# Half of K computed by seven products beside w2's, kept in DRAM and loaded back in attention

## The chip, the cores and the metric

One core of a Trainium2 chip runs the whole program. The metric is the device time of one execution in microseconds (us); a kernel's time is the median of several runs. The core's engines work at the same time and meet through semaphores: TensorE (PE) multiplies and writes into the eight accumulator banks, VectorE (DVE) and ScalarE (ACT) read the banks and do elementwise work, GpSimd (POOL) does some elementwise work, and SyncE (SP) issues nearly all DMAs. Each engine takes its instructions in the order in which the program gives them; an instruction that waits holds up everything behind it on that engine.

## What is computed

The reference, cut to what matters here (x has 2048 rows of 1024, four segments of 512 rows; 32 heads of 32; F is 3584):

```python
xn = _layernorm(A_x, axis=-1)
# branch A, attention with a memory that goes from segment to segment
q, k, v = xn @ wq, xn @ wk, xn @ wv                # split into heads and segments
for s in range(N):
    logits = einsum('bhqd,bhkd->bhqk', qs, ks) * scale + mask
    p = softmax(logits); a_dot = p @ vs
    pq = phi(qs)                                   # t + 1 where t > 0, else exp(t)
    a_mem = (pq @ M) / (pq @ z + 1e-6)
    o = g * a_mem + (1.0 - g) * a_dot              # g = sigmoid(beta)
    pk = phi(ks); M = M + pk.T @ vs; z = z + pk.sum()
A = o @ wo
# branch B, an MLP over the rows
h = _layernorm(xn); u = gelu(einsum('bsd,sf->bdf', h, w1) + b1)
B = transpose(einsum('bdf,fs->bds', u, w2) + b2)
out = x + A + B
```

## The kernel before

The kernel is one Python program that gives instructions to the engines in the order in which it runs; the class FW adds the semaphore waits (L134) from what each instruction reads and writes. There is no other scheduler: the order of the calls is the order on every engine.

**Hidden layer and w2.** `norm_and_first_hidden` loads x, normalises it chunk by chunk (a chunk is 128 rows, `N_TCH` = 16 of them) and multiplies the first two column blocks. A few matmuls on zeros run ahead of it (`N_WARM`, L389). `products` (about L703) then works through 20 *pairs*: 12 of w1 (indices 0 to 11) and 8 of w2 (12 to 19, called w2 pairs 0 to 7 here). A pair is a product of 2 by 2 blocks in seven block products instead of eight, in the order 1, 6, 5, 7, 2, 4, 3 (`ORDER`). Left operands are blocks of the weights or one of four sums of them (`sums`, on VectorE), right operands are blocks of the activations or one of four differences (`differences`, VectorE). A product of w2 is 14 matmuls of 512 columns. Three banks take a pair's results: X products 1 and 2, Y products 6, 7 and 4, Z products 5 and 3. Between them banks are read while they go on accumulating: ScalarE copies X after product 1 (`copy_bank`), VectorE adds Y to that copy after product 6 and after product 7 (`add_bank`, L690), so product 7 can start only when the add after product 6 has read Y. `after2` finishes w2's results (L934), stores them as partial outputs, loads the next w2 columns, and issues the next pair's four sums, one after each of products 7, 2, 4 and 3. The sums of consecutive w2 pairs lie in two sets in turn (`alloc_s2`).

**x for attention.** x is loaded again chunk by chunk (`xn_load`), normalised on VectorE (`xn_scale`, L986) and transposed by a DMA (`xn_transpose`) into xnT. Two buffers xs take the chunks in turn, so a load waits until the transpose of two chunks before has landed. Chunks 0 to 3 go through in w2 pairs 0 to 3, one a pair; the other twelve in attention, in the first four units of segments 0 to 2.

**Attention.** `attention` (about L1354) runs over 32 *units*; a unit is four heads of one segment, units 0 to 7 are segment 0, 8 to 15 segment 1 and so on. Each unit has logits (row-packed matmuls into banks 0 to 3, an exp on ScalarE, L1216, a mask on GpSimd, L1220), and the weighing of V by the unit before's probabilities in three parts (`weigh`, banks 4 and 5, read out by VectorE, L1267). Between these pieces `dense` puts matmuls of *jobs*, eight 512-column matmuls each, in banks 6 and 7 in turn: q and k of the unit after next, one of V's chunks, and output products wo of an earlier segment. `unit_jobs` says which; `cut` divides them among the gaps. k is copied out by VectorE (L1112), q by ScalarE (L1103). VectorE's other work (`combine`, L1298 to L1320, `phi_q` and `phi_k`, L1080 and L1082, scaling x) stands in a list `side`; one piece of it is issued whenever a job reaches one of its *stops* (`STOPS`, after matmuls 1, 4 and 7, or 1 and 4 where VectorE reads the job's bank). `wo_plan` says in which units the output products stand. `tail` does the last segment's output products, in the banks of a fixed list.

Of the kernel before, what the change touches and what calls it, by code (L numbers as in the profile page):

```python
# [105 lines left out]
class FW:  # L106
    N_DMA_SEMS = 64
    N_OUT_SEMS = 44
    N_OWN_SEMS = 16
# [275 lines left out]
class _Kernel:  # L385
# [3 lines left out]
    N_WARM = 12  # L389
# [314 lines left out]
    def products(self):  # L704
        fw = self.fw
        g = _Walk(self.mem, self.G_AT, self.B_AT)
        for b in range(8):
            if b == 0:
                self.alloc_hidden(g)
            self.gelu(b // 2, b % 2, self.bank(b), self.R_bank[b])  # L710
        self.h_diff((1, 2))
        self.pairs = {}
        n1 = self.N_W1
        order = [(0, 1), (1, 1), (0, 2), (1, 2), (0, 6), (0, 5), (0, 7), (1, 6), (0, 4), (1, 5), (1, 7), (0, 3), (1, 4), (1, 3)]
        order += [(i, p) for i in range(2, n1 + self.N_W2) for p in self.ORDER]
        self.later = deque()
        for i, p in order:
            if i not in self.pairs:
                self.begin_pair(i)
            pair = self.pairs[i]  # L720
            self.product(pair, p)
            pair.done.add(p)
            (self.after1 if i < n1 else self.after2)(pair, p)
# [29 lines left out]
    def begin_pair(self, i):  # L753
        n1 = self.N_W1
        banks = [(3 * i + j) % 8 for j in range(3)]
        if i < n1:
            slot, R_slot, s, R_s, n = self.w1s[i % 2], self.R_w1s[i % 2], self.s1[i % 2], self.R_s1[i % 2], N_TCH // 2
            blocks, R_b, t, R_t = self.h, self.R_h, self.hT, self.R_hT
        else:
            k = (i - n1) % 2  # L760
            slot, R_slot, s, R_s, n = self.w2s[k], self.R_w2s[k], self.s2[k], self.R_s2[k], N_FCH // 2
            blocks, R_b, t, R_t = self.gB, self.R_gB, self.gT, self.R_gT
        v = slot[:].rearrange("p (j k) f -> p k j f", k=2)
# [18 lines left out]
        pair.t = [3 * (i % 2) + j for j in range(3)]  # L782
        pair.done = set()

    def pair_sums(self, i, ks):
        if i < self.N_W1 + self.N_W2:
            if i not in self.pairs:
                self.begin_pair(i)
            pair = self.pairs[i]
            for k in ks:  # L790
                self.sums(k, pair.a, pair.R_a, pair.s, pair.R_s)
# [70 lines left out]
    S2_AT = (38912 + 256, 53248 + 256)  # L862
# [10 lines left out]
    def alloc_s2(self, k):  # L873
        self.s2[k], self.R_s2[k] = self.mem.take(f"sum2_{k}", [P, 4, N_FCH // 2, P], F16, self.B_AT + self.S2_AT[k], 4)

    def alloc_w2_first(self):
        self.w2s, self.R_w2s, self.s2, self.R_s2 = [None] * 2, [None] * 2, [None] * 2, [None] * 2
        self.alloc_w2(0)
        self.load_w2(0)

    def alloc_s2_first(self):
        self.alloc_s2(0)

    def alloc_w2_rest(self):
        self.alloc_w2(1)
        self.load_w2(1)
        self.alloc_s2(1)
        w = _Walk(self.mem, self.B_AT + self.STG_AT, self.B_AT + self.S2_AT[0])
# [5 lines left out]
        w = _Walk(self.mem, self.B_AT + self.FREE_AT, self.SB_END - self.SB_BASE)  # L894
        self.xnT, self.R_xnT = [None] * 2, [None] * 2
        self.xnT[0], self.R_xnT[0] = w.take("xnT0", [P, N_DCH, SEG_L], BF16, 4)
# [5 lines left out]
        for name, src in (("wq", self.A_wq), ("wk", self.A_wk)):  # L902
# [6 lines left out]
            for u in range(N_UNIT):  # L909
# [3 lines left out]
        for k in range(2):  # L913
            self.load_stg(k)
# [4 lines left out]
    def after2(self, pair, p):  # L919
# [20 lines left out]
        elif p == 6:  # L940
# [4 lines left out]
            if i < 4:  # L945
                self.xn_load(i)
# [6 lines left out]
        elif p == 2:  # L953
            finish("X", 0, 0, None)
            if i < 4:
                self.xn_scale(i)
        elif p == 4:
# [4 lines left out]
            if i < 4:  # L962
                self.xn_transpose(i)
# [9 lines left out]
        elif p == 3:  # L973
            self.pair_sums(pair.k + 1, (4,))
        if i == self.N_W2 - 1:
# [8 lines left out]
    def xn_scale(self, c):  # L984
        x, R = self.xs[c % 2], self.R_xs[c % 2]
        self.fw.op("dve", lambda e: e.tensor_scalar(x[:], x[:], self.ln_mv[:, c, 0:1], self.ln_rs[:, c, 0:1],  # L986
# [131 lines left out]
    def proj_job(self, ring, u, end):  # L1118
# [10 lines left out]
        stops = self.STOPS if end.__qualname__.startswith("_Kernel.q_job") else self.STOPS_DVE  # L1129
        return [0, None, lambda: [ring.res[u % 2]] + self.R_xnT[s % 2], mm, finish, stops]  # L1130

    def v_job(self, m, c):
# [14 lines left out]
        return [0, None, lambda: [self.R_wv[bv], self.R_xnT[s % 2][c]], mm, end, self.STOPS_DVE if m in (1, 2) else self.STOPS]  # L1147

    def wo_job(self, c, half):
# [14 lines left out]
        return [0, None, lambda: [self.R_wo] + self.R_oT[s % 2], mm, end, self.STOPS if c >= 9 else self.STOPS_DVE]  # L1164
# [6 lines left out]
    def dense(self, n, side=True):  # L1171
        fw = self.fw
        while n > 0 and self.jobs:
            job = self.jobs[0]
            at, b, reads, mm, end, stops = job
            if not side:
                stops = ()
# [165 lines left out]
    STOPS, STOPS_DVE = (1, 4, 7), (1, 4)  # L1343

    def unit_jobs(self, u):
# [4 lines left out]
        if u + 2 < N_UNIT:  # L1350
            jobs += [self.q_job(u + 2), self.k_job(u + 2)]
        return jobs

    def attention(self):  # L1354
        self.jobs, self.turn = deque(), 0
        self.side = deque()
        self.exps, self.in_etmp = [], [None] * 4
        self.wo_plan = {}
        for s in range(N_SEG - 1):
            at = [N_GRP * s + 10 + n for n in range(8)] if s < 2 else [27, 28, 29, 30, 30, 31, 31, 31]  # L1360
# [11 lines left out]
        for u in range(N_UNIT):  # L1372
# [7 lines left out]
            if u < 10:  # L1380
# [3 lines left out]
            end = u >= N_UNIT - 4  # L1384
            self.dense(cuts[0])
# [29 lines left out]
            self.dense(100)  # L1415
        while self.side:
# [12 lines left out]
    def tail(self):  # L1429
# [6 lines left out]
        def product(n, j0, j1, cols=((0, 512),)):  # L1436
            i, h, b = n // 2, n % 2, (6, 7, 0, 1, 2, 3, 5, 4)[n]
# [63 lines left out]
```

The softmax here doesn't subtract the row's maximum and nothing guards it: scores larger than these inputs give would overflow.

## Time and profile before

| what | us |
|---|---|
| median of 3 runs (lowest, highest) | 657.46 (657.33, 657.51) |
| profiled execution, its own time | 659.62 |
| its span, first to last instruction | 657.9 |
| mean granted TensorE clock | 0.997 |
| first w2 product starts | 181.8 |
| first attention job starts | 351.1 |
| unit 0, 8, 16, 24 start (first logits) | 365.0, 424.1, 497.6, 573.5 |
| unit 31 starts | 631.8 |

Times inside the profile are counted from the start of the span. Busy times of the engines by stage, in us:

| stretch | PE | DVE | ACT | POOL | DMA share |
|---|---|---|---|---|---|
| 200.0 to 230.0 (w2) | 30.00 | 13.01 | 1.19 | 4.23 | 0.68 |
| 230.0 to 280.0 (w2) | 50.00 | 19.62 | 1.19 | 8.87 | 0.63 |
| 409.1 to 424.1 (units 6, 7) | 15.02 | 9.42 | 11.96 | 5.57 | 0.58 |
| 478.6 to 497.6 (units 14, 15) | 18.98 | 16.03 | 13.42 | 6.43 | 0.50 |
| 573.5 to 592.2 (units 24, 25) | 18.70 | 14.43 | 12.38 | 6.41 | 0.42 |

A busy PE says little by itself: a 512-column matmul is recorded as 379 ns, but the next one starts 216 ns later. Rows of the profile name an instruction by line, engine, operation and its tiles (what is written, an arrow, what is read); a helper's line stands for every call of it, L198 for all matmuls and L220 for all DMAs.

### The profile page before, as it was taken

To read this page: it belongs to the slowest core of one execution; us is meant where nothing else is said; L and a number is where in the kernel's file an instruction comes from. 1 tells how busy PE (TensorE), PEld (TensorE's weight loads), DVE (VectorE), ACT (ScalarE), POOL (GpSimd) and SP (SyncE) were. 2 spreads that over 40 slices of the span, in tenths; PEclk is the share of its full clock that TensorE was granted. 3 is DMA by queue.
4 is the path that set the end of the run, shared out by engine and by line. 5 is a ranking of instruction groups with operands and counts; after the bars stand their busy time and mean duration, and the time that the engine had idled before them with its cause. 6 is when DMAs were issued, how large, how long until landed. Compare 5 with 4: busy or idle time off the path is not lost.

```text
span 657.9 us, 11118 instructions
## 1 busy us (share of the span) xinstructions
PE 648.8 (99%) x4624; PEld 303.1 (46%) x4624; DVE 426.7 (65%) x821; ACT 275.9 (42%) x297; POOL 146.6 (22%) x181
## 2 busy tenths in 40 slices
PE   7999999999999999999999999999999999999988
PEld 3444444444444444444444445554454554444444
DVE  6965676665644553344422476589888998877895
ACT  7542232232210000000011777887667766767750
POOL 2500000000011222022220243333233333333440
PEclk8999999999999999999999999999999999999999
DMA  8704233242556546854386586568644784445424
GB/s 305 208 0 129 65 93 100 64 115 78 132 172 179 153 122 170 181 156 117 96 220 200 152 174 132 104 155 160 130 94 116 176 171 116 118 97 83 80 81 137
DMA packets 187242, 87.65 MB, mean 133 GB/s; under 512 B 116024, under 2 KB 174392, under 8 KB 187192
## 3 DMA queue, kind: packets, MB, share of 16 engines
q1 hardware_dynamic: 187048, 86.91, 53.3%
q8 instruction: 36, 0.59, 0.4%
q14 instruction: 14, 0.11, 0.1%
q10 hardware_dynamic: 144, 0.03, 0.0%
HBM read 67.13 MB, written 8.39 MB: 115 GB/s over the span
## 4 chain that ended last, share of the span: by engine, by line
PE 92%; DVE 6%; issue 1%; DMA 1%; ACT 0%; SPq 0%; DVEq 0%
PE ps_all L198 92%; DVE prod L1314 1%; DVE fin L1158 1%; DMA xin<-in_A_x_dram 1%; DVE fin L1448 1%; DVE ost L1267 0%; DVE mtmp L1082 0%; DVE mtmp L1080 0%; DVE o_s L1320 0%; DVE pqT L1082 0%; ACT pT L1216 0%; DVE srec L1309 0%; DVE xs L986 0%; DVE kT L1112 0%; DVE srec L1308 0%
## 5 line engine op out<-in xcount | busy, mean ns | idle before, releaser
L1216 ACT ACTIVATE pT<-ps_all 128x2048 bf16<-128x2048 f32 x80 | 150.1, 1876 | 55.4 <-PE ps_all L198 55.3
L1220 POOL TENSOR_SCALAR_AFFINE_SELECT pT<-pT 128x512 bf16<-128x512 bf16 x128 | 98.1, 783 | 195.5 <-ACT pT L1216 195.5
L690 DVE TENSOR_TENSOR part<-ps_all,part 128x512 f32<-128x512 f32 x76 | 52.5, 691 | 119.0 <-PE ps_all L198 118.2
L926 POOL TENSOR_TENSOR part<-part,stg 128x512 f32<-128x512 f32 x24 | 33.0, 1401 | 266.2 <-DVE part L690 266.2
L695 ACT ACTIVATE part<-ps_all 128x512 f32<-128x512 f32 x20 | 11.9, 597 | 149.0 <-PE ps_all L198 149.0
L198 PE MATMUL ps_all<-wv,xnT 128*128 128x512 bf16 x256 | 68.5, 380 | 0.9 <-DVE kT L1112 0.9
L742 ACT ACTIVATE g<-part,b1c 128x512 f16<-128x512 f32 x36 | 26.0, 722 | 98.9 <-DVE part L690 98.9
L198 PE MATMUL ps_all<-wo,oT 128*128 128x512 bf16 (+2 forms) x272 | 65.8, 367 | 1.2 <-DVE fin L1158 1.2
L198 PE MATMUL ps_all<-xnT,wq 128*128 128x512 bf16 x256 | 63.6, 380 | 0.0
L198 PE MATMUL ps_all<-xnT,wk 128*128 128x512 bf16 x256 | 61.8, 380 | 0.0
L1267 DVE CAST ost<-ps_all 128x396 bf16<-128x396 f32 (+2 forms) x96 | 44.6, 475 | 25.3 <-PE ps_all L198 24.0
L198 PEld LDWEIGHTS ps_all<-vA,pT 128*128 128x128 bf16 x1280 | 45.4, 96 | 20.4 <-DVE ost L1267 3.9
L198 PE MATMUL ps_all<-g,w2s 128*128 128x512 f16 x224 | 51.0, 379 | 0.0
L198 PE MATMUL ps_all<-g,sum 128*128 128x512 f16 x224 | 51.0, 379 | 0.0
L198 PE MATMUL ps_all<-gT,sum 128*128 128x512 f16 x224 | 49.7, 379 | 0.0
L198 PE MATMUL ps_all<-vA,pT 128*128 128x33 bf16 x1280 | 48.6, 178 | 0.4 <-DVE ost L1267 0.3
L198 PE MATMUL ps_all<-h,sum 128*128 128x512 f16 x192 | 45.2, 379 | 0.0
L198 PE MATMUL ps_all<-h,w1s 128*128 128x512 f16 x192 | 44.9, 379 | 0.0
L198 PE MATMUL ps_all<-hT,sum 128*128 128x512 f16 x192 | 43.6, 379 | 0.0
L1314 DVE TENSOR_TENSOR prod<-ost,srec 128x512 bf16<-128x512 bf16 x48 | 40.9, 852 | 0.8
L198 PEld LDWEIGHTS ps_all<-xnT,wk 128*128 128x128 bf16 x256 | 23.8, 98 | 29.8 <-issue 3.2
L198 PEld LDWEIGHTS ps_all<-wo,oT 128*128 128x128 bf16 x272 | 23.5, 97 | 25.9 <-issue 5.4
(99 smaller groups left out, 804.5 us busy)
## 6 DMA issues: line engine op xcount, KB each, us to landing
w2s<-in_B_w_dram SPq DMA_DIRECT2D x8, 1792.0 KB, 8.6
w1s<-in_B_w_dram SPq DMA_DIRECT2D x12, 1024.0 KB, 5.6
wq<-in_A_wq_dram SPq DMA_DIRECT2D x32, 256.0 KB, 3.3
wk<-in_A_wk_dram SPq DMA_DIRECT2D x32, 256.0 KB, 3.3
stg<-in_A_x_dram SPq DMA_DIRECT2D x16, 256.0 KB, 3.0
xs<-in_A_x_dram SPq DMA_DIRECT2D x16, 256.0 KB, 3.4
out_dram<-stg SPq DMA_DIRECT2D x16, 256.0 KB, 2.9
fin<-out_dram SPq DMA_DIRECT2D x16, 256.0 KB, 3.6
```

What stands on the lines that cost most here:

```text
L198: ins = self.nc.tensor.matmul(*args, **kwargs)
L690: self.fw.op("dve", lambda e: e.tensor_tensor(self.tmp[dst][:], self.bank(b), self.tmp[src][:], op=ALU.add), reads=[self.R_bank[b], self.R ...
L695: self.fw.op("act", lambda e: e.activation(self.tmp[dst][:], self.bank(b), ACT.Copy), reads=[self.R_bank[b]], writes=[self.R_tmp[dst]])
L742: self.fw.op("act", lambda e: e.activation(self.gB[f % 2][half][:, f // 2, :], src, ACT.Gelu_apprx_tanh, bias=self.b1c[:, f:f + 1], scale= ...
L926: fw.op("pool", lambda e: e.tensor_tensor(self.tmp[t][:], self.tmp[t][:], self.stg[k][:, 512 * half:512 * half + 512], op=ALU.add), reads= ...
L1158: self.fw.op("dve", lambda e: e.tensor_tensor(dst, self.bank(b), dst.bitcast(F16), op=ALU.add), reads=[self.R_bank[b], R], writes=[R])
L1216: fw.op("act", lambda e: e.activation(dst, src, ACT.Exp, scale=SCALE), reads=self.R_bank[0:4], writes=[R[v % 2][kb] for v, kb, _ in blocks ...
L1220: fw.op("pool", lambda e: e.affine_select(d, d, pattern=[[0, 4], [1, P]], compare_op=ALU.is_ge, fill=0.0, base=0, channel_multiplier=-1), ...
L1267: fw.op("dve", lambda e: e.tensor_copy(dst, src), reads=[self.R_bank[b]], writes=[self.R_ost[o][part]])
L1314: fw.op("dve", lambda e: e.tensor_tensor(self.prod[:, n, :], ost[:, n, 0:D_HEAD], rec[:, n].unsqueeze(2).to_broadcast([P, 16, D_HEAD]), op ...
L1448: fw.op("dve", lambda e: e.tensor_tensor(dst, self.ps[:, b, c0:c1], dst.bitcast(F16), op=ALU.add), reads=[self.R_bank[b], R], writes=[R])
```

## The change

K of segments 2 and 3 (units 16 to 31) is no longer computed by attention's k jobs. Four *K pairs* of seven products, four matmuls each, are put between the w2 pairs: after w2 pairs 2, 3, 4 and 5. Each makes K of 256 of the 1024 columns for both segments; the results go to a DRAM tensor `k_part` in 16 blocks of 128 KB, and attention loads one block for each unit (`k_load`), two units ahead. For this chunks 8 to 15 of x are loaded, scaled and transposed (as 16-bit floats) in w2 pairs 0 and 1, the four differences of x are made in w2 pair 2, and the sums of wk in the pair before each K pair. Chunks 8 to 15 still go through attention as before for Q and V. Chunks 0 to 3 move from w2 pairs 0 to 3 to pairs 6 and 7. All w2 pairs use one set of sums, and the buffers of the K pairs lie in the other set's place and in that of attention's buffers, which are allocated after the last K pair. In attention the jobs of a unit with at most 26 dense matmuls have more stops; three of segment 2's eight wo products stand one unit earlier; the tail's products take the banks in another order; there are 14 warm-up matmuls in place of 12, and more semaphores for DMAs (60 and 24 in place of 44 and 16).

```diff
-    N_WARM = 12
+    N_WARM = 14
@@ products
-        order += [(i, p) for i in range(2, n1 + self.N_W2) for p in self.ORDER]
+        keys = list(range(n1 + self.N_W2))
+        for g in range(self.N_KP):
+            keys.insert(n1 + self.K_FIRST + 2 * g, ("k", g))
+        self.seq = {i: n for n, i in enumerate(keys)}
+        order += [(i, p) for i in keys[2:] for p in self.ORDER]
...
-            (self.after1 if i < n1 else self.after2)(pair, p)
+            (self.after_k if isinstance(i, tuple) else self.after1 if i < n1 else self.after2)(pair, p)
@@ begin_pair
-        banks = [(3 * i + j) % 8 for j in range(3)]
+        banks = [(3 * self.seq[i] + j) % 8 for j in range(3)]
+        if isinstance(i, tuple):
+            slot, R_slot, s, R_s, n = self.wkp, self.R_wkp, self.sk, self.R_sk, N_DCH // 2
+            blocks, R_b, t, R_t = self.kB, self.R_kB, self.kD, self.R_kD
+            halves = "p (k j) f -> p k j f"
...
+    N_KP, K_FIRST = N_GRP // 2, 3
...
+    def after_k(self, pair, p):
+        fw = self.fw
+        g = pair.k[1]
+        t1, t2, t3 = pair.t
+
+        def put(acc, row, col, t):
+            n, b = 2 * row + col, pair.bank[acc]
+            dst, R = self.kout[n], self.R_kout[n]
+            if t is None:
+                fw.op("act", lambda e: e.activation(dst[:], self.bank(b), ACT.Copy), reads=[self.R_bank[b]], writes=[R])
+            else:
+                fw.op("dve", lambda e: e.tensor_tensor(dst[:], self.bank(b), self.tmp[t][:], op=ALU.add),
+                      reads=[self.R_bank[b], self.R_tmp[t]], writes=[R])
+            v = N_GRP * col + 2 * g + row
+            fw.dma(self.k_d[v], dst[:], reads=[R], writes=[self.R_kd[v]], is_output=True)
+
+        if p == 1:
+            self.copy_bank(pair, "X", t1)
+        elif p == 6:
+            self.add_bank(pair, "Y", t2, t1)
+        elif p == 7:
+            self.add_bank(pair, "Y", t3, t1)
+            put("Z", 1, 1, t3)
+        elif p == 2:
+            put("X", 0, 0, None)
+        elif p == 4:
+            put("Y", 1, 0, t1)
+            if g + 1 < self.N_KP:
+                self.load_wkp(g + 1)
+        elif p == 3:
+            put("Z", 0, 1, t2)
+            if g == self.N_KP - 1:
+                self.alloc_attention()
+
+    def k_prepare(self, i, p):
+
+        n = self.ORDER.index(p)
+        if i < 2:
+            c = 8 + 4 * i
+            if n in (2, 3, 4, 5):
+                m = n - 2
+                self.xn_scale(c + m, F16)
+                s, cc = (c + m) // 4, m
+                x = self.xs[m % 2]
+                self.fw.dma(self.xnK[s - 2][:, :, cc * P:(cc + 1) * P], x[:].bitcast(F16), reads=[self.R_xs[m % 2]],
+                            writes=[self.R_xnK[s - 2][cc]], transpose=True, own=True)
+            if n < 4:
+                self.xn_load(c + n)
+        g = i - self.K_FIRST + 1
+        if g == 0 and n < 4:
+            self.differences(self.kB, self.R_kB, self.kD, self.R_kD, (n + 1,))
+        if 0 <= g < self.N_KP and n in (4, 5):
+            self.pair_sums(("k", g), ((1, 2), (3, 4))[n - 4])
@@ after2
-            if i < 4:
-                self.xn_load(i)
...
-            if i < 4:
-                self.xn_scale(i)
...
-            if i < 4:
-                self.xn_transpose(i)
...
+        self.k_prepare(i, p)
+        if i >= self.N_W2 - 2:
+            c = 2 * (i - self.N_W2 + 2)
+            if p in (1, 6):
+                self.xn_load(c + (p == 6))
+            elif p in (5, 7):
+                self.xn_scale(c + (p == 7))
+                self.xn_transpose(c + (p == 7))
@@ dense
-            at, b, reads, mm, end, stops = job
-            if not side:
-                stops = ()
+            at, b, reads, mm, end, on_dve = job
+            stops = self.stops[on_dve] if side else ()
...
-    STOPS, STOPS_DVE = (1, 4, 7), (1, 4)
+    STOPS = ((1, 4, 7), (1, 4))
+    STOPS_FEW = ((1, 3, 5, 7), (1, 3, 5))
@@ unit_jobs
-            jobs += [self.q_job(u + 2), self.k_job(u + 2)]
+            jobs.append(self.q_job(u + 2))
+            if u + 2 < N_UNIT // 2:
+                jobs.append(self.k_job(u + 2))
+            else:
+                self.k_load(u + 2)
...
+    def k_load(self, u):
+        k, v = u % 3, u - N_UNIT // 2
+        self.fw.dma(self.kT[k][:], self.k_d[v], reads=[self.R_kd[v]], writes=[self.R_kT[k]])
@@ attention
-            at = [N_GRP * s + 10 + n for n in range(8)] if s < 2 else [27, 28, 29, 30, 30, 31, 31, 31]
+            at = [N_GRP * s + 10 + n for n in range(8)] if s < 2 else [27, 28, 28, 29, 30, 30, 31, 31]
...
-            if u < 10:
+            if total <= 26:
...
+            self.stops = self.STOPS_FEW if total <= 26 and u >= N_GRP else self.STOPS
...
+            if N_UNIT // 2 <= u + 2 < 3 * N_GRP:
+                self.exps.append((1, self.kT[(u + 2) % 3], self.R_kT[(u + 2) % 3], u + 2))
@@ tail
-            i, h, b = n // 2, n % 2, (6, 7, 0, 1, 2, 3, 5, 4)[n]
+            i, h, b = n // 2, n % 2, (0, 1, 2, 3, 6, 7, 5, 4)[n]
```

## The prediction

> **What bounds the kernel now.** First the page's busy times and its chain of waits:
>
> ```profile
> PE 648.8 (99%) x4624; PEld 303.1 (46%) x4624; DVE 426.7 (65%) x821; ACT 275.9 (42%) x297; POOL 146.6 (22%) x181
> ...
> PE 92%; DVE 6%; issue 1%; DMA 1%; ACT 0%; SPq 0%; DVEq 0%
> ```
>
> TensorE is the chain almost everywhere, so a matmul counts at its start-to-start distance, not at its 379 ns. TensorE's timeline at the end of w2 gives that:
>
> ```profile
> 348.11 3.18 PE L198 MATMUL ps_all<-g,sum 128*128 128x512 f16 x14
> 351.13 1.89 PE L198 MATMUL ps_all<-xnT,wq 128*128 128x512 bf16 x8
> ```
>
> 14 matmuls in 351.13 - 348.11 = 3.02 us, 0.2157 each. Next, who has room in attention. These are stretches of two units each (columns: busy time of PE, PEld, DVE, ACT, POOL, then clock, DMA share, GB/s):
>
> ```profile
> 458.69:478.64 19.95, 19.10 (x194) 9.36 (x195) 17.95 (x36) 13.41 (x13) 5.65 (x9) 1.00 0.64 127
> ...
> 497.62:516.59 18.97, 18.97 (x193) 9.26 (x192) 16.38 (x36) 13.41 (x13) 6.43 (x9) 1.00 0.58 150
> 516.59:535.57 18.98, 18.98 (x194) 9.28 (x194) 17.29 (x37) 13.41 (x13) 6.58 (x9) 1.00 0.80 144
> ...
> 592.22:608.95 16.73, 16.73 (x177) 8.09 (x176) 12.57 (x26) 12.38 (x11) 6.38 (x9) 1.00 0.56 83
> ```
>
> VectorE is busy for 16.4 to 18 of 19 us. At 17.95 the stretch is 0.97 longer than its neighbour: there TensorE already waited for it. Last, the queue in which w2 loads and transposes stand (SP's timeline, then two landings, the last column):
>
> ```profile
> 201.17 0.35 SPq L220 DMA_DIRECT2D out_dram<-stg  x1
> 201.56 0.43 SPq L220 DMA_DIRECT2D w2s<-in_B_w_dram  x1
> 202.04 6.30 SPq L220 DMA_TRANSPOSE xnT<-xs  x1
> 208.39 0.56 SPq L220 DMA_DIRECT2D out_dram<-stg  x1
> 211.83 0.80 SPq L220 DMA_DIRECT2D stg<-in_A_x_dram  x2
> 212.67 0.43 SPq L220 DMA_DIRECT2D xs<-in_A_x_dram  x1
> ```
> ```profile
> w2s<-in_B_w_dram SPq DMA_DIRECT2D x1, 1792.0 KB, 8.8
> ```
> ```profile
> xnT<-xs SPq DMA_TRANSPOSE x1, 9.1
> ```
>
> A transpose issued right behind a w2 load holds SP for 6.3 us and lands at 211.1, 9.5 after that load's issue; one issued with an empty queue holds SP for 1.3 and lands after 3.0 to 5.0 (median of all 4.0).
>
> **Part by part.** *Matmuls.* Removed: 16 k jobs of 8, 128 x 0.2157 = 27.61. Added: 4 K pairs x 7 products x 4 = 112 x 0.2157 = 24.16. Net -3.45 us, all on the path.
>
> *Inside a K pair.* Products last 0.86 us, w2's 3.02. At its start VectorE still finishes the w2 pair before: by that pair's rows (eviction 0.2 us after the product, 0.67, then a sum of 1.08) it is free 1.95 after the K pair's start. The add that product seven needs (0.69) then ends at 2.64; product seven was due at 2.59. Its add, the first eviction and the next add follow at 0.6 to 0.7 each, so product four waits about 0.1 more. With semaphores I take 0.28 a pair, 1.1 us in all (bounds 0, if all hides, and 4 x 0.7 = 2.8, one add late in each).
>
> *Preparing x for K.* Eight chunks (8 to 15) are loaded, scaled and transposed in w2 pairs 0 and 1, through two xs buffers: load, scale, transpose, and only then that buffer's next load. VectorE (8 x 0.7 for scales, 4 x 1.15 for differences, half of the 2.29 for 4096 columns, 16 small sums of about 0.4) has the room: in a w2 pair it waits 4.29 and 5.35 us for TensorE. But it takes its work in order, and SP does too. By the clock of the trace before, with pair 1 starting at 203.07 and pair 2 at 224.22:
> scale 9 follows the sum after product seven, ends 198.8; transpose 9 lands 3.7 later, 202.6. Load 11 waits for it; transpose 10 leaves SP at 204.4, pair 2's w2 load goes out at 204.8 (201.56 before). Transpose 11 stands behind it: SP is held to 211.6, it lands at 214.3. Load 12 goes at 212.2, lands 216.0 (3.4 plus that queue); two stg loads wait for chunk 0's store (2.6 after 212.0), load 13 for transpose 11: 215.9. Scale 12 ends 216.7, transpose 12 lands 221.0, load 14 lands 224.5; transpose 13 (SP free at 221.5) lands 225.2, load 15 leaves. Transpose 14 leaves SP at 227.0, pair 3's w2 load at 227.4, and transpose 15 behind it lands 9.5 later, 236.9.
> The first difference for K is queued on VectorE after pair 2's product one and waits for all eight transposes. Behind it stands the add for product six; product seven waits for that add, because it accumulates in the same bank. So 236.9 + 1.2 + 0.7 = 238.7 against 233.29, when product seven was due: +5.4 us. Floor: pair 3's w2 load waits for pair 1's product four (221.2, eviction and store to 222.6), so transpose 15 lands at 232.1 at best, and 0.7 us is left. Top: transposes 11 and 15 land after 11.4 (the worst row) in place of 9.1: 10 us.
>
> The Trainium skill (DMA: Bandwidth & Descriptors, Queues, rings and completion order) says that completion is not in order of issue. If a transpose overtook the w2 load, this wait would be about 2 us; the row, 211.1 against the load's 210.4, says it does not.
>
> *The clock after that wait.* TensorE's start, then its granted clock in stretches of 2 us (the third figure from the end; the figure before it is PE's busy time):
>
> ```profile
> 1.25 4.12 PE L198 MATMUL ps_all<-warm 128*128 128x512 bf16 x12 [1.25 <-DVE brow L501]
> 7.47 6.78 PE L198 MATMUL ps_all<-h,w1early 128*128 128x512 f16 x23 [2.11 <-DVE h L628]
> ```
> ```profile
> 6.00:8.00 2.00, 0.53 (x2) 0.86 1.02 337
> 8.00:10.00 2.00, 2.00 (x7) 0.50 1.01 358
> 10.00:12.00 2.00, 2.00 (x9) 0.79 1.08 389
> ```
>
> After 2.1 us of idleness the clock is 0.50 for 3.4 us, 7.4 to 10.8, and 8 matmuls start 0.427 apart: 8 x 0.21 = 1.7 us lost. An idle time of 5.4 us should cost that again, less what of the slow stretch falls into the idleness: 1.3 (0 to 1.7).
> *Two more warm-up matmuls* fill 2 x 0.2157 of that first gap and end before the first h. They cost nothing, and gain 0 (taken: the gap shrinks by a fifth only) to 1.7, if the clock stays up.
>
> The Trainium skill (TensorE: Matmul & The Clock Gate, What's actually happening) lets the clock fall after an idle window of about 3.4 us. By it a gap of 2.1 us need not cost anything; the row shows that it did, so the window was judged on partial idleness.
>
> *Attention, units 14 to 23.* A stretch of two units falls from 18.97 to 18.97 - 16 x 0.2157 = 15.52. VectorE loses two kT copies, 1.37. Before it needed 16.38 busy and about 0.5 of short gaps (18.97 - 16.38 - 2.1 spent waiting for TensorE); so 15.5 stays, 16.4 in the stretch at 516.59, 15.2 in the lightest: about 78 over five stretches against 77.6. It becomes an equal bound and has no slack left, though its side work is spread over more stops. Between 0 and 0.97 a stretch (the row at 458.69) I take 0.4: 2.0 us.
> *Units 24 to 31.* Unit 26 has 16 dense matmuls left between its exps (1.88 each). Over units 26 and 27 ScalarE needs 12.38 of 13.28. Taken 1.0, bounds 0 and 2 (one exp).
> *K through DRAM.* 16 loads of 128 KB replace 16 wk loads of 256 KB; a 128 KB store takes 1.7, the load is issued more than a unit (7 us) ahead of its logits, so nothing; if SP were held up longer than that, logits would wait. Stores of K stand in SP's order behind evictions that have happened, while w2 loads are a pair ahead: nothing. *One set of sums*: each is rewritten after its last reader, four products ahead of need; without that cover 1.1 a sum. *Chunks 0 to 3 in pairs 6 and 7*: transpose 3 stands behind wv (two loads, 7.4 each to land) but has 9 us until the first q job; cover gone, up to 3.
> *Tail.* The first tail product waited 1.17 for a fin eviction on VectorE to free bank 6; bank 0 waits for the last exp instead, about 0.4: -0.8 (0 to -1.2).
>
> **Sum:** -3.45 + 1.1 + 5.4 + 1.3 + 2.0 + 1.0 - 0.8 = +6.55. The profiled execution took 659.62 (span 657.9), and so 666.2; the runs' median is 657.46, 2.2 less, and so **664.0**.
>
> **Rivals.** *Chunks arrive in time* (the other side): loads and transposes overlap better than I chain them, transpose 15 lands before 231.4 and pair 2 does not wait; attention keeps half its waits. -3.45 + 1.1 + 1.0 + 0.5 - 0.8 = -1.65: 655.8. For it: the page's DMA digits are 4 to 8 in w2, so the engines are not full. Against: two buffers, and the w2 load ahead of transposes 11 and 15. It decides when pair 2's product seven starts less than 2 us late.
> *VectorE rules attention*: 0.97 lost in each of the ten units, 9.7 in place of 2.0: 671.7. For it the row at 458.69; against, 16 copies fewer, and those were what TensorE waited for there.
> *A short wait*: half of 5.4, no clock loss, half the attention waits: -3.45 + 1.1 + 2.7 + 1.5 - 0.8 = +1.05: 658.5.
>
> **From these to numbers.** Forecast 0.60 (660.5 to 668.5), chunks in time 0.20, VectorE rules 0.10, short wait 0.10. A run tells 0.2%, 1.3 us, from no change. Faster: 0.16 of the second case. Same: its other 0.04 and half of the last, 0.09. Slower: 0.75. The range 655.5 to 669.5 leaves out about half of each outer case, some 0.15.
>
> **What would show it.** In the profile after: a gap in TensorE of about 5 us in the third w2 pair before a g,sum product, VectorE's first K difference waiting for an xnK transpose, and a clock of 0.5 behind it; two-unit stretches from 478 on of 15.5 to 16 us with VectorE above 95%; bank 0's product less than 0.5 late. No gap in the third pair, or stretches above 17 us, would prove me wrong.

## The result, and the profile after

| what | us |
|---|---|
| median of 4 runs after (lowest, highest) | 675.44 (675.28, 676.56) |
| median of 4 runs before beside them | 657.39 (657.23, 657.51) |
| ratio after to before, 95% interval | 1.0278 (1.0261 to 1.0296) |
| profiled execution after, its own time; its span | 675.5; 673.8 |

The change costs 18.05 us; 6.5 were forecast. By span it is 15.9 us, since the profiled execution of before had lost about 2 us at its start that its timed runs do not lose (see the fourth experiment). The page's busy times and its chain of waits after the change:

```profile
PE 643.2 (95%) x4559; PEld 301.9 (45%) x4610; DVE 449.6 (67%) x853; ACT 281.1 (42%) x305; POOL 147.3 (22%) x181
...
PE 48%; DVE 12%; issue 3%; ACT 1%; DMA 1%; DVEq 0%
```

TensorE is busy 5.6 us less and falls from 99 to 95% of a longer span. (The change removes 14 matmuls, worth 3.0 us; this profile lacks records of some 50 matmuls, 4559 against 4610 weight loads, so the 5.6 is rough.) The followed chain now leaves TensorE for VectorE again and again (its shares add up to less than one span, so they serve only to say which engine takes over). Where TensorE waits in w2 is seen in its timeline, w2 pairs 1 and 2 and the first K pair:

```profile
217.66 3.19 PE L198 MATMUL ps_all<-gT,w2s 128*128 128x512 f16 x14 [1.35 <-DVE part L690]
...
240.06 5.01 PE L198 MATMUL ps_all<-g,sum 128*128 128x512 f16 x14 [7.11 <-DVE part L690]
...
258.29 1.04 PE L198 MATMUL ps_all<-xnK,sumk 128*128 128x512 f16 x4 [1.57 <-DVE part L690]
```

Each of the three waits is for `add_bank` on VectorE: product seven waits until the add after product six has read its bank. The longest is the one forecast, before product seven of w2 pair 2. VectorE's timeline says why the add was late:

```profile
216.46 0.55 DVE L1087 TENSOR_SCALAR xs<-xs,ln_mv,ln_rs 128x1024 f16<-128x1024 bf16 x1 [8.49 <-DMA xs<-in_A_x_dram]
216.92 0.69 DVE L690 TENSOR_TENSOR part<-ps_all,part 128x512 f32<-128x512 f32 x1
...
238.17 1.23 DVE L664 TENSOR_TENSOR kD<-xnK,xnK 128x2048 f16<-128x2048 f16 x1 [7.84 <-issue]
239.31 0.68 DVE L690 TENSOR_TENSOR part<-ps_all,part 128x512 f32<-128x512 f32 x1
...
249.01 2.17 DVE L664 TENSOR_TENSOR kD<-xnK,kD 128x2048 f16<-128x2048 f16 x1
```

At 216.46 VectorE had sat 8.49 us in front of the scale of chunk 12, with pair 1's add queued behind it. At 238.17 it had sat 7.84 us in front of the first difference of K (the profile names no releaser), with pair 2's add behind that. What both were late for stands in SP's queue:

```profile
202.83 0.45 SPq L220 DMA_DIRECT2D w2s<-in_B_w_dram  x1
203.82 7.19 SPq L220 DMA_TRANSPOSE xnK<-xs  x1
...
211.68 0.43 SPq L220 DMA_DIRECT2D xs<-in_A_x_dram  x1
...
227.60 0.45 SPq L220 DMA_DIRECT2D w2s<-in_B_w_dram  x1
228.71 6.70 SPq L220 DMA_TRANSPOSE xnK<-xs  x1
235.47 0.57 SPq L220 DMA_DIRECT2D out_dram<-stg  x1
```

The transposes of chunks 11 and 15, issued right behind a w2 load, hold SP for 7.19 and 6.70 us; chunk 12's load leaves at 211.68 only, and the first difference starts 2.8 us after transpose 15 has left SP. TensorE's clock after the long wait (stretches of 2 us; PE's busy time, then the granted clock):

```profile
236.00:238.00 2.00, 0.00 (x0) 0.74 0.92 237
238.00:240.00 2.00, 0.00 (x0) 0.50 0.21 27
240.00:242.00 2.00, 1.94 (x5) 0.50 0.61 236
242.00:244.00 2.00, 2.00 (x6) 0.56 0.00 0
```

The clock is halved at about 236.9 and returns at about 243.8: the 14 matmuls behind the wait go from 240.06 to 244.91, 4.85 us instead of 3.02.

The attention, by stretches of two units (columns as in the prediction): units 14 and 15, 16 and 17, 18 and 19, then 26 and 27, then unit 30 alone.

```profile
513.92:529.52 15.60, 15.24 (x176) 7.74 (x179) 14.67 (x33) 12.97 (x12) 5.54 (x8) 1.00 0.39 97
529.52:546.41 16.89, 15.46 (x174) 7.74 (x177) 15.92 (x34) 13.45 (x13) 6.75 (x9) 1.00 0.48 113
546.41:563.83 17.42, 15.47 (x176) 7.75 (x179) 16.45 (x35) 13.47 (x14) 6.73 (x9) 1.00 0.74 174
...
612.48:626.47 13.99, 13.05 (x158) 6.53 (x161) 11.44 (x24) 12.37 (x12) 6.18 (x9) 1.00 0.35 78
640.07:648.76 8.69, 7.03 (x84) 3.25 (x86) 7.61 (x15) 6.54 (x5) 4.03 (x5) 1.00 0.13 37
```

TensorE's own work in a stretch is 15.5; the three take 15.60, 16.89 and 17.42, VectorE busy for 94% of each. All five stretches of units 14 to 23 take 83.31 us (513.92 to 597.23) where five times 15.52 is 77.6. In unit 30 TensorE is busy for 7.03 of 8.69.

From stage starts in the two traces, the whole of the 15.9 us by span:

| stage | before | after | difference | of it matmuls |
|---|---|---|---|---|
| start to first w2 product | 181.79 | 179.88 | -1.9 | 0 |
| w2 and K, to the first attention job | 169.34 | 206.66 | +37.3 | +24.16 |
| attention, to the last matmul's start | 303.8 | 283.4 | -20.4 | -27.61 |
| last matmul's start to the span's end | 2.9 | 3.8 | +0.9 | 0 |

So the w2 part lost 13.1 us beyond its matmuls, the attention 7.2, the end 0.9. The w2 part differs from one execution to the next: in the seven profiles whose program leaves it as the change made it, it takes 205.0 to 206.7 us, and the one above is the longest. Differences of a microsecond between such kernels are therefore read from the stage that an edit touches, not from the total.

### The profile page after: what moved, and what is told of

Read it like the earlier page. It is cut to its first block, busy times and chain, and to the rows that moved or that the text cites. A ratio compares the mean times of both kernels' runs of the same rounds, so it can differ in the third digit from the quotient of the medians.

```text
span 673.8 us, 11152 instructions
## 1 busy us (share of the span) xinstructions
PE 643.2 (95%) x4559; PEld 301.9 (45%) x4610; DVE 449.6 (67%) x853; ACT 281.1 (42%) x305; POOL 147.3 (22%) x181
## 4 chain that ended last, share of the span: by engine, by line
PE 48%; DVE 12%; issue 3%; ACT 1%; DMA 1%; DVEq 0%
PE ps_all L198 48%; DVE prod L1413 3%; DVE ost L1366 2%; DVE pqT L1183 1%; ACT pT L1315 1%; DVE mtmp L1181 1%; DVE fin L1258 1%; DVE mtmp L1183 1%; DVE srec L1408 1%; DMA oT<-o_s 1%; DVE fin L1559 1%; DVE MZbf L1376 0%; DVE srec L1409 0%; DVE xs L1087 0%; DVE sum L649 0%
## 5 line engine op out<-in xcount | busy, mean ns | idle before, releaser
L690 DVE TENSOR_TENSOR part<-ps_all,part 128x512 f32<-128x512 f32 x84 | 58.0, 691 | 109.7 <-PE ps_all L198 108.9
L695 ACT ACTIVATE part<-ps_all 128x512 f32<-128x512 f32 x24 | 14.3, 597 | 168.1 <-PE ps_all L198 168.1
L198 PE MATMUL ps_all<-wv,xnT 128*128 128x512 bf16 x241 | 63.3, 380 | 1.4 <-DVE kT L1213 0.8
L198 PE MATMUL ps_all<-wo,oT 128*128 128x512 bf16 (+2 forms) x257 | 62.7, 366 | 1.2 <-DMA oT<-o_s 0.3
L198 PE MATMUL ps_all<-xnT,wq 128*128 128x512 bf16 x241 | 60.6, 379 | 1.3 <-issue 1.1
L198 PE MATMUL ps_all<-g,sum 128*128 128x512 f16 x224 | 52.8, 389 | 7.1 <-DVE part L690 7.1
L198 PEld LDWEIGHTS ps_all<-vA,pT 128*128 128x128 bf16 x1280 | 45.0, 96 | 27.9 <-DVE ost L1366 13.4
L1413 DVE TENSOR_TENSOR prod<-ost,srec 128x512 bf16<-128x512 bf16 x48 | 45.9, 956 | 0.8
L198 PEld LDWEIGHTS ps_all<-g,sum 128*128 128x128 f16 x224 | 22.2, 100 | 35.2 <-DVE part L690 7.6
L198 PE MATMUL ps_all<-qT,kT 32*128 32x384 bf16 (+3 forms) x512 | 31.7, 301 | 3.8 <-ACT pT L1315 1.9
L198 PEld LDWEIGHTS ps_all<-xnT,wq 128*128 128x128 bf16 x256 | 22.9, 97 | 27.3 <-issue 4.4
```

What stands on the lines that cost most here:

```text
L198: ins = self.nc.tensor.matmul(*args, **kwargs)
L690: self.fw.op("dve", lambda e: e.tensor_tensor(self.tmp[dst][:], self.bank(b), self.tmp[src][:], op=ALU.add), reads=[self.R_bank[b], self.R ...
L695: self.fw.op("act", lambda e: e.activation(self.tmp[dst][:], self.bank(b), ACT.Copy), reads=[self.R_bank[b]], writes=[self.R_tmp[dst]])
L1413: fw.op("dve", lambda e: e.tensor_tensor(self.prod[:, n, :], ost[:, n, 0:D_HEAD], rec[:, n].unsqueeze(2).to_broadcast([P, 16, D_HEAD]), op ...
```

## The experiments

Every run was timed beside the kernel before on the same chip; before was 657.4 to 657.5 in all of them.

**w2 loads behind the transposes.**

```diff
-            if i + 2 < self.N_W2:
+            if 2 <= i and i + 2 < self.N_W2:
                 self.load_w2(i + 2)
...
         self.k_prepare(i, p)
+        if i < 2 and p == 4:
+            self.load_w2(i + 2)
```

> The changed kernel (675.4), but the w2 loads of pairs 2 and 3 are issued behind the transposes of chunks 11 and 15 and not ahead of them. Theory, the queue order makes the wait in w2: both transposes land about 4 us after their issue, the gap of 7.1 before product seven in w2 pair 2 falls to 0 to 2.5, the 1.35 in pair 1 and the 1.8 of slow clock behind the gap go, total 665 to 668. Rival, the chain through two buffers is too long whatever stands in the queue: the gap stays above 5, total above 672.

Measured 666.79 us, ratio 1.014 (1.0127 to 1.0154), inside the theory's range: 8.65 us come back from the order of two pairs of DMAs. TensorE in this kernel:

```profile
233.21 3.20 PE L198 MATMUL ps_all<-g,sum 128*128 128x512 f16 x14 [1.50 <-DVE part L690]
...
249.62 1.04 PE L198 MATMUL ps_all<-xnK,sumk 128*128 128x512 f16 x4 [1.56 <-DVE part L690]
```

The 7.11 are 1.50, 14 matmuls take 3.20 again, and pair 1 shows no wait. The first K pair's wait is unchanged, so it has another cause.

**No masks in units 14 to 23**, and **no min in phi of k**. Two ways to take work off VectorE there without touching TensorE: the first leaves GpSimd's masks out, the second an operation of VectorE.

```diff
         for v, kb, _ in blocks:
+            if 14 <= v <= 23:
+                continue
```
```diff
+        if k == 1 and 15 <= u <= 23:
+            fw.op("dve", lambda e: e.scalar_tensor_tensor(dst, src, 1.0, et[:], op0=ALU.add, op1=ALU.max),
+                  reads=[R_src, R_et], writes=[R_dst])
+            return
```

> The changed kernel without GpSimd's causal masks in units 14 to 23 (their probabilities are not masked). Theory, VectorE is the bound there and its operations grew slower because GpSimd's masks now fall on more of them: prod falls from 1035 to about 700 ns, the five two-unit stretches from 513.9 to 597.2 shrink from 83.3 to 78 or 79, total 670 to 671. Rival, VectorE has too much work at any speed, or TensorE waits for something else: stretches stay above 82, total above 674.

> The changed kernel without the minimum with 1 in phi of k for units 15 to 23, nine VectorE operations of 0.39 us less (phi is wrong where k is positive). Theory, VectorE's total is the bound in units 14 to 23: 3 to 4 us less, 671.5 to 672.5. Rival, what counts is only where the weighing's eviction stands in VectorE's order: under 1 us, 674.5 or more.

Measured 668.78 us, ratio 1.0172 (1.0159 to 1.0186), faster than the 670 to 671 expected, and 672.11 us, ratio 1.0226 (1.021 to 1.0241). Of the 6.7 us that the first gives back, 5.4 lie in units 14 to 23, which now take 77.9 us (513.23 to 591.12). Without masks units 16 to 19 read:

```profile
528.73:544.23 15.50, 15.14 (x174) 7.82 (x176) 13.66 (x34) 13.37 (x14) 0.00 (x0) 1.00 0.52 116
544.23:559.73 15.50, 15.14 (x174) 7.83 (x176) 14.11 (x35) 13.37 (x14) 0.00 (x0) 1.00 0.81 189
```

The same 35 VectorE instructions that took 16.45 us now take 14.11, and TensorE sets the 15.50. The instruction that shrinks most is `prod`; the answers for its tile, after and without masks (durations minimum/median/maximum):

```profile
L1413 DVE TENSOR_TENSOR prod<-ost,srec x20: 692/1060/1143, 513.0 to 596.9; 128x512 bf16<-128x512 bf16 x20
```
```profile
L1415 DVE TENSOR_TENSOR prod<-ost,srec x20: 682/688/1003, 512.3 to 590.7; 128x512 bf16<-128x512 bf16 x20
```

The Trainium skill (SBUF — State Buffer, Who interferes with whom) has a VectorE instruction with two SBUF inputs and a GpSimd instruction that reads SBUF share a port, the later one waiting for the earlier. The medians, 0.69 without masks and 1.06 beside them, agree with that in direction. In the kernel before the median was 1.00 already, so `prod` is only a part of what grew with the change.

ScalarE needs about 13.4 us in either kernel, and at 13.37 of 15.50 it holds nothing. Without the min, 3.3 us come back; 2.5 of them lie in units 14 to 23 by the stage starts (80.84 for 83.31, with 3.1 us less of VectorE's work), the rest is in the w2 part, which that edit does not touch. So the total falls where the theory put it, but the stage gives less than its 3 to 4 us.

**Two more warm-up matmuls alone**, in the kernel before.

```diff
-    N_WARM = 12
+    N_WARM = 14
```

> The kernel before with 14 warm-up matmuls in place of 12, nothing else. Theory, the profiled execution of before lost 1.9 us to a half clock at its start and the timed ones did not (it was 2.2 us longer than they): no change, 657.4. Rival, all executions of before lose it and 14 keep the clock up: 655.5.

Measured 657.39 us, ratio 0.9998 (0.9989 to 1.0007). Its profiled execution has no half clock at the start and a span of 655.8. A profile of before with only its last waits changed (below), and so with 12 warm-up matmuls, has no half clock there either and spans 656.0. So the 1.7 us that the forecast read from the trace before are lost in single executions: of 21 runs of before beside the last experiments, one took 659.73 us, at a mean granted clock of 0.997; the others lie between 657.2 and 657.8.

**The first K pair's sums first, its differences behind the adds**, on top of the first experiment.

```diff
-        if g == 0 and n < 4:
-            self.differences(self.kB, self.R_kB, self.kD, self.R_kD, (n + 1,))
-        if 0 <= g < self.N_KP and n in (4, 5):
+        if g == 0 and n == 0:
+            self.pair_sums(("k", 0), (1, 2, 3, 4))
+        if g == 0 and n in (1, 2, 3):
+            self.differences(self.kB, self.R_kB, self.kD, self.R_kD, ((1, 2), (3,), (4,))[n - 1])
+        if 0 < g < self.N_KP and n in (4, 5):
```

> The kernel with both w2 loads behind the transposes (666.8 us), with the four sums of the first K pair ahead of the differences, and the four differences behind the adds after products six, five and seven of w2 pair 2. Theory (the 1.57 us in the first K pair are VectorE's queue: a difference of 2.17 us and four sums between the adds; and 1.5 us before pair 2's product seven is the add behind the first difference): both go, 664.0 us (663.5 to 665.0). Rival (the wait is on the differences themselves, since chunk 15 arrives too late for any order): product five of the first K pair now waits for its difference, 666 to 668 us.

Measured 664.41 us, ratio 1.0107 (1.009 to 1.0124): 2.4 us less than 666.79. The same two products:

```profile
232.60 3.20 PE L198 MATMUL ps_all<-g,sum 128*128 128x512 f16 x14 [0.92 <-DVE part L690]
...
247.83 1.04 PE L198 MATMUL ps_all<-xnK,sumk 128*128 128x512 f16 x4 [0.38 <-DVE part L690]
```

The K pair's wait was queueing on VectorE; it falls from 1.56 to 0.38 with the same work in another order. Pair 2's falls to 0.92 only; what holds the rest is not shown.

**The end of the attention as before**, and **the tail's banks as before**, each alone in the changed kernel.

```diff
-            at = [...] if s < 2 else [27, 28, 28, 29, 30, 30, 31, 31]
+            at = [...] if s < 2 else [27, 28, 29, 30, 30, 31, 31, 31]
...
-            if total <= 26:
+            if total <= 26 and u < 3 * N_GRP:
...
-            self.stops = self.STOPS_FEW if total <= 26 and u >= N_GRP else self.STOPS
+            self.stops = self.STOPS_FEW if total <= 26 and N_GRP <= u < 3 * N_GRP else self.STOPS
...
```
```diff
-            i, h, b = n // 2, n % 2, (0, 1, 2, 3, 6, 7, 5, 4)[n]
+            i, h, b = n // 2, n % 2, (6, 7, 0, 1, 2, 3, 5, 4)[n]
```

> The changed kernel (675.4 us) with the end of the attention as before the change: out-projection jobs over units 27 to 31 as 1, 1, 1, 2, 3, the five cuts and the three stops of before in units 24 to 31; K still loaded. Theory (unit 30 took 1.1 us more and the end 0.6 us more than their TensorE work because of the new places of the out-projection jobs and the finer stops): 674.0 us (673.4 to 674.8). Rival (they come from VectorE's and ScalarE's work per unit, which is the same with fewer matmuls beside it): 675.4 us (675.0 to 677).

> The changed kernel (675.4 us) with the tail's products in the banks of before (6, 7, 0, 1, 2, 3, 5, 4). My forecast gave the new banks 0.8 us: 676.2 us (675.8 to 676.6) without them. Rival (the tail's first products wait for the last exponentials to leave banks 0 and 1 instead, so that the new banks cost as much as they give): 675.4 us or less (674.6 to 675.6).

Measured 675.58 us, ratio 1.0276 (1.0261 to 1.0292), and 675.42 us, ratio 1.0274 (1.0259 to 1.029): neither moves the time. The places of the output products are not what the end lost: from the start of unit 24 to the span's end it takes 77.65 us with the old ones and 76.54 with the new. For the banks the times cannot tell. In the traces the tail's first product waits 0.74 us for an add on VectorE with the old banks and 0.24 for an exp with the new, and from the start of unit 31 to the start of the last products (663.52 in the changed kernel) it takes 15.9 and 14.8 us; but in the profiled execution with the old banks the w2 part happened to be 1.2 us shorter.

**No masks in units 24 to 31.** The edit of the second experiment with `if v >= 24`.

> The changed kernel (675.4 us) without GpSimd's causal masks in units 24 to 31 (so the weights above the diagonal are left in). Theory (the end of the attention, 1.7 us over its TensorE work in units 26 to 31 and the tail, is VectorE's work grown beside the masks, as in units 14 to 23): 674.0 us (673.3 to 674.6). Rival (ScalarE, 12.4 us of exponentials and copies in the 14.0 us of units 26 and 27, or the order of the out-projection jobs): 675.4 us (674.8 to 676).

Measured 673.71 us, ratio 1.0247 (1.0233 to 1.0261), 1.7 us back; by stage starts 1.2 of it lie behind the start of unit 24. Unit 30 takes 7.91 in place of 8.69 (639.98 to 647.89). In the changed kernel its weighing waited for a copy on VectorE:

```profile
643.21 0.57 PE L198 MATMUL ps_all<-vA,pT 128*128 128x33 bf16 x16 [0.77 <-DVE ost L1366]
646.38 0.40 PE L198 MATMUL ps_all<-qT,kT 32*128 32x256 bf16 x8 [0.58 <-ACT pT L1315]
```

Without masks the first wait is gone and the second, for ScalarE's exp, is still 0.58. VectorE again, then, for 0.8 of the 1.9 us that units 24 to 30 lost.

**phi of K of segment 2 beside w2's products**, on top of the order above: exp, min and max run on the K pair's output in the w2 part, a transpose and a store follow, and the attention loads the result. One exp of ScalarE and a min and a max of VectorE leave each of units 16 to 23.

```diff
+        def k_phi(row):
+            e_, m_, R = self.xs[row][:, :SEG_L], self.xs[row][:, SEG_L:], self.R_xs[row]
+            k, v = self.kout[2 * row], 2 * g + row
+            fw.op("dve", lambda e: e.tensor_scalar(e_, e_, 1.0, None, op0=ALU.min), reads=[R], writes=[R])
+            fw.op("dve", lambda e: e.scalar_tensor_tensor(m_, k[:], 1.0, e_, op0=ALU.add, op1=ALU.max),
+                  reads=[self.R_kout[2 * row], R], writes=[R])
+            fw.dma(e_.rearrange("p (a b) -> p a b", a=4), m_, reads=[R], writes=[R], transpose=True, own=True)
+            fw.dma(self.kp_d[v], e_, reads=[R], writes=[self.R_kpd[v]], is_output=True)
...
     def k_transpose(self, u):
+        if N_UNIT // 2 <= u < 3 * N_GRP:
+            v = u - N_UNIT // 2
+            self.fw.dma(self.pk[u % 2][:].rearrange("p a b -> p (a b)"), self.kp_d[v], reads=[self.R_kpd[v]],
+                        writes=[self.R_pk[u % 2]])
```

> The kernel with the w2 loads behind the transposes and the first K pair's sums and differences in the other order (664.4 us), and phi of K of segment 2 worked out beside w2's products too: ScalarE's exp and VectorE's two operations of units 16 to 23 leave the attention, and the weights' source is transposed in the w2 part, stored and loaded back. Theory (units 14 to 23 are bound by VectorE's total, 78.5 us of work against 77.6 on TensorE): some 9.4 us of VectorE work leave, the five stretches fall from 83.3 to about 78, 659.2 us (658.3 to 660.7). Rival (those stretches are held by single casts that come late, or by ScalarE, not by VectorE's total): at most 1.5 us come back, 662.9 us or more. If the added work in the w2 part is not free, waits of up to 4 us appear there behind the K pairs.

Measured 658.14 us, ratio 1.0012 (1.0003 to 1.0021): 6.3 us less than 664.41, and just under the theory's range. Units 16 to 19, then 26 and 27:

```profile
517.29:532.77 15.48, 15.48 (x178) 7.87 (x178) 13.83 (x30) 12.43 (x12) 6.36 (x9) 1.00 0.51 128
532.77:548.25 15.48, 15.48 (x178) 7.78 (x178) 14.58 (x31) 12.43 (x12) 6.24 (x9) 1.00 0.80 189
...
594.45:608.45 14.00, 13.42 (x162) 6.53 (x162) 11.45 (x24) 12.38 (x12) 6.20 (x9) 1.00 0.33 78
```

With its masks, but four VectorE instructions fewer in a stretch, TensorE is busy from end to end in units 16 to 19, and the five stretches take 77.5. The w2 part did not pay for the moved work: there the wait of pair 2 is gone.

**A shorter row of waits at the end.** The edit: SyncE waits at the end only for those stores that it has not already waited for. Counted from the programs, the row is 38 waits long before, 54 after and 62 with phi moved, and 10 in all three with the edit (the 44, 60 and 68 of the expectations are the semaphores set aside). In the changed kernel, in the best one so far, and in the kernel before:

```diff
-        sp = self.E["sp"].eng
         for t in self.out_toks:
-            sp.wait_ge(t.sem, t.val)
+            self.E["sp"].wait_tok(t)
```

> The changed kernel (675.4 us), whose SyncE at the end waits only for the stores that it has not waited for already: the 16 partial results and the 16 stores of K drop out of 60 waits in a row. Theory (the span goes on 3.1 us behind VectorE's last add where it was 2.2 before, because the change puts 16 waits more into that row): 0.9 us or a little more come back, 674.3 us (673.8 to 674.8). Rival (the last store's way to memory ends the span, 1.6 us after its issue, and the waits run beside it): 675.4 us (674.9 to 676).

> The kernel with the w2 loads behind the transposes, the other order of sums and differences, and phi of K of segment 2 beside w2's products (658.1 us), with the same shorter row of waits (24 of 68 stores fewer in it are K's and phi's, 16 the partial results). If the row of waits is what the end pays: 656.9 us (656.3 to 657.6), under the kernel before. If not: 658.1 us (657.6 to 658.6).

> The kernel before (657.5 us) with the same edit: 16 of its 44 waits drop out. Its last store lands about 1.6 us behind its issue at 656.3 us, 0.3 us ahead of the span's end, so at most 0.3 us can come back by either theory: 657.4 us (657.0 to 657.8).

Measured 673.76 us, ratio 1.0249 (1.0235 to 1.0263); 657.47 us, ratio 0.9999 (0.999 to 1.0008); 657.68 us, ratio 0.9998 (0.9989 to 1.0007). The last DMA issue in the changed kernel, and in the same kernel with the shorter row:

```profile
670.50 0.37 ACTq L220 DMA_DIRECT2D out_dram<-fin  x1
```
```profile
669.37 0.37 ACTq L220 DMA_DIRECT2D out_dram<-fin  x1
```

The spans end at 673.8 and 671.7: 2.9 and 2.0 us behind the issue's end. Before it was 2.0, with 38 waits (655.49 + 0.37 to 657.9). So the longer row, 54 waits for 38, costs 0.9 us after all work was done. (The waits themselves are not in the profile. A small load of instructions also falls into the last half microsecond of the changed kernel, and into neither of the two others, so how the 0.9 divides is not shown.) The other 0.8 of the 1.7 that came back is not the row's: by stage starts the w2 part of this execution is 1.6 us shorter than in the changed kernel's profile, at the other end of the scatter named above. (The wait of 1.35 in w2 pair 1 is absent here. It stands in two of the seven profiles with this w2 part, and where it is absent pair 2's is 6.6 to 7.7 long.)

The kernel with all repairs is as fast as the kernel before, not faster. In its profile the 3.45 us of matmuls that the change saves are met by 1.8 us that the w2 part still takes beyond its matmuls (179.44 to 374.74) and by 1.1 in the attention (374.74 to 652.10).

## Why the prediction was wrong

The direction and the main mechanism held: two transposes stuck behind w2 loads, the first difference late, the add behind it, the half clock. The sizes did not, and one sign that the prediction itself named as proof against it came: a stretch above 17 us (17.42, units 18 and 19). Term by term, from the traces (a wait is counted from the time at which the product was due by matmul starts, which makes it some 0.2 longer than the idle time shown in the rows):

| term | forecast | measured |
|---|---|---|
| matmuls | -3.45 | -3.45 |
| inside the four K pairs | +1.1 | +0.8 |
| wait before pair 2's product seven | +5.4 | +7.3 |
| wait in pair 1 (not in every run) | none | +1.5 |
| first K pair's wait, beyond the others' | none | +1.6 |
| clock behind the wait | +1.3 | +1.8 |
| units 14 to 23 | +2.0 | +5.7 |
| units 24 to 30 | +1.0 | +1.9 |
| unit 31 and tail | -0.8 | -0.3 |
| row of waits at the end | none | +0.9 |
| sum | +6.55 | +17.75 |

The stage starts give 15.9 + 1.9 = 17.8, with the start that before's profiled execution lost; the medians 18.05.

**Two steps failed. The largest miss in one term is "about 78 over five stretches against 77.6".** From it the prediction took 2.0 us, with 0 to 0.97 a stretch as bounds; 5.7 is 1.1 a stretch, outside them. Its 78 were 75.5 of busy time, before's less the copies, and 0.5 of short gaps in each stretch. Measured are 78.5 busy and 4.8 of gaps, 1.0 in each. Why the gaps doubled is not shown. The busy time grew because durations of before do not carry over: in a shorter unit the same instructions meet GpSimd's masks elsewhere. The min of phi in these units, before and after:

```profile
L1080 DVE TENSOR_SCALAR mtmp<-etmp x20: 280/285/288, 479.4 to 570.9; 128x512 bf16<-128x512 bf16 x20
```
```profile
L1181 DVE TENSOR_SCALAR mtmp<-etmp x20: 280/286/723, 514.7 to 595.9; 128x512 bf16<-128x512 bf16 x20
```

Before, none of the 20 ran beside a mask and none took over 288 ns. After, five run beside one for more than half a microsecond and take 717 to 723; the other 15 take 280 to 288. Without masks (second experiment) the longest takes 290. The second rival, 9.7 us lost there, named VectorE as the bound but took another price; 5.7 lies about midway between it and the forecast. The kernel with phi moved shows that it is VectorE's total: with 8.5 us less to do (70.0 busy) the loss is gone, masks and all. ScalarE loses work there too, but without masks the loss was gone with ScalarE's work unchanged.

**The other: the wait in w2 was worked out along the right chain, but for one product only.** Together the waits there are 10.4 us for 5.4. The w2 load of pair 2 left at 202.83 (forecast 204.8), yet chunk 12's load left at 211.68 (forecast 212.2) and the last transpose left SP at 235.4 and landed at 237.9 (forecast 236.9), while product seven was due 0.5 earlier than forecast (232.78 for 233.29); 7.3 was inside the stated top of 10. Not priced was that each late or long item holds up every add behind it: chunk 12's scale stood in front of pair 1's add, and the fourth difference (2.17 us) and the first pair's four sums stood in front of the K pair's adds. "Inside a K pair" counted VectorE's load in an undisturbed pair, without them. This wait does not come from pair 2's: it stays at 1.56 where that one falls to 1.50, and goes when the same work is put in another order. The other three K pairs lose 0.2 each, less than the 0.28 assumed.

**The clock** behaved as forecast and the size was near, 1.8 for 1.3; it differs by execution, from 1.4 to 2.5 in the seven profiles with this wait. That the two warm-ups cost and gain nothing was right. The 2.2 us between the profiled execution and the median was taken off correctly.

**The tail's 0.8** is not settled. Against before, 0.3 us is left of it between the start of unit 31 and the last products. Against the changed kernel with the old banks the first product's wait is 0.5 shorter and that stretch 1.1, in one execution of each; the timed runs show no difference.

**The end's row of waits** was in no term. "K through DRAM: nothing" priced the way of the data, not the 16 semaphores that a final wait is made for.

**The rival on the other side**, chunks in time, needed only the two w2 loads behind the transposes to come true; even so the kernel was at 666.8, since its 655.8 also assumed half of an attention loss that was already too small, and had nothing for the first K pair's wait and the row of waits.

## What to carry to other kernels

Before handing TensorE's products to a stage where VectorE is 86% busy, count VectorE's time per unit at the new, shorter unit, with what GpSimd does beside it; matmuls removed below that bound give nothing back. When a late transfer feeds an engine that works in order, price every instruction queued behind the wait, not only the first consumer, and put a big prefetch behind the small transfer that is needed next. What a change adds to a final or common wait costs time too.

## What was not expected of the hardware

- The clock fell about 4.0 us after TensorE went idle (the last matmul's record ends at about 232.95, the clock is halved at 236.94), stayed at half through the rest of the gap, and came back about 3.7 us after work resumed. These two times are not fixed: over the seven profiles with this wait (6.6 to 7.7 us idle) they are 2.5 to 4.8 and 2.8 to 5.1. The slow stretch itself lasted 6.83 us in six of them and 10.24 in one, twice and three times the 3.41 of the slow start before. A wait of 1.5 us in the first experiment's kernel left the clock alone, while the 2.11 us of idleness at the start of before did not. The Trainium skill (TensorE: Matmul & The Clock Gate, What's actually happening) gives windows of about 3.4 us both ways; the rows here lie around that.
- It is not only a transpose that SP cannot pass on behind a w2 load: in the first experiment's kernel a plain 256 KB store stands there, and its issue holds SP for 4.19 us (0.57 for such a store at 235.47 above).

```profile
205.44 0.58 SPq L220 DMA_DIRECT2D w2s<-in_B_w_dram  x1
206.06 4.19 SPq L220 DMA_DIRECT2D out_dram<-stg  x1
```

- A row of waits on semaphores long since raised can end the program. From SP's last issue to the span's end it is 1.6 us with 38 waits (656.3 to 657.9), 2.5 with 54 (671.3 to 673.8) and 1.6 again with 10 (670.1 to 671.7).
